# Attention output turned by DMA in bf16 and normalised one unit at a time, with GpSimd's time counted by the program

## The chip, the cores and the metric

The kernel runs on one core of one Trainium2 chip. The metric is the device time of one execution in microseconds (us). The engines that matter are TensorE (PE; its weight loads are PEld), VectorE (DVE), ScalarE (ACT), GpSimd (POOL), and the queue of SyncE (SP), from which every DMA of this kernel is issued.

## The reference

One transformer block without biases, in bf16, for 2048 tokens of width 512: an attention block with 32 heads of 16 columns, then a gated FFN of width 1792. Both start with a layer norm and end with a residual addition.

```python
def _A_ref(x, wqkv, wo):                       # x: (1, 2048, 512), already normalised
    qkv = (x @ wqkv).reshape(B, S, 3, H, Dh).transpose(2, 0, 3, 1, 4)   # H = 32, Dh = 16
    q, k, v = qkv[0], qkv[1], qkv[2]
    scores = jnp.einsum("bhqd,bhkd->bhqk", q, k) * (Dh ** -0.5)
    p = softmax(scores, axis=-1)
    o = jnp.einsum("bhqk,bhkd->bhqd", p, v)
    return o.transpose(0, 2, 1, 3).reshape(B, S, D) @ wo

def _B_ref(x, w_gate, w_up, w_down):           # F = 1792
    return (gelu_tanh(x @ w_gate) * (x @ w_up)) @ w_down

h  = x + _A_ref(layernorm(x), A_wqkv, A_wo)
h2 = h + _B_ref(layernorm(h), B_w_gate, B_w_up, B_w_down)
```

## The kernel before, in words

**Units, groups and ticks.** The queries are cut into 8 groups of 256 tokens (`gi`, 0 to 7; `GL` = 7 is the last), the heads into 8 slots of 4 heads. A unit is one group and one slot; there are 64 (`NU`), in the order of the groups. One Python loop writes the program in ticks. A unit has 16 ticks, so the first 1024 ticks carry the first pass over the scores and the last ones, up to tick 1048, the rest of the second pass, which runs 24 ticks behind (`P2_START`). All engines get fixed lists; waits are semaphores that the planner (`Plan`) puts in.

**First pass.** In each tick TensorE makes two score tiles of 128 queries by 512 keys (L797) and VectorE takes their row maxima in one reduction of 128x1024 elements (L806). GpSimd folds the maxima of a unit: a part after the second and the third quarter of the keys (`negm_part`, emitted in ticks 8 and 12 of the unit), the rest in tick 15 (`negm_pre`, L832 to L840), which leaves the negative maxima as three bf16 rows in `ST`. `negm_post` turns them with a DMA transpose (L846, `STG<-ST`) and, `ADDX` = 4 ticks later, GpSimd adds them to the rows of Q that carry the maximum (L851). Tick 24 of the unit is the first that reads them.

**Second pass.** In each tick TensorE makes two transposed score tiles of 128 keys (L867), and ScalarE evaluates exp into the ring of probability tiles (L896; in the last 24 ticks two tiles at once, L884). `item_pv` (L910) multiplies by V, to which a column of ones is attached, so the sum of the exponentials comes out as 17th row of each head.

**What becomes of a unit's output before.** `item_pv` ends in ticks 8 to 11 of a unit. ScalarE copies its bank to `OA` in fp32. After every second unit `item_ofin` runs: TensorE turns the pair in four fp32 transposes (L936), ScalarE copies the 17 columns of each head to `OAT`, and GpSimd takes the reciprocal of the sums as a power of -1 (L945, `LINV`) and multiplies (L949) into `Otok`. `slot_done` counts the slots; when a group has its eight, `post_onT` turns `Otok` by DMA for the output projection `item_oproj` (L1015); then follow a layer norm from sums (Square on ScalarE, L1029; GpSimd, L1039 to L1053), a DMA transpose (`post_hnT`, L1005) and, three ticks later, the group's FFN is queued: seven pairs of `item_gate` and `item_up` (L1089, 16 matmuls for a pair) and two `item_down` (L1139, 14 matmuls and the residual L1144), one for each 128 tokens.

**The dense stream.** All these items (`Dense`) go through one generator that adds a piece in each tick: items with a due time (`prio`: PV, turning, output projection) first, FFN items in their order. A piece is two to four matmuls' worth; where a tick has less, dummy matmuls (L1299) fill it. A gate or up may start only where an estimate of ScalarE's lag is at most `LAG_START` and where it ends before the next due item. The estimate grows by the cost given to each copy or tangent and falls in each tick:

```python
def act_tick(exps):
    act_lag[0] = max(0.0, act_lag[0] + 0.478 * exps - 1.135)      # exps is 2
```

A copy of a gate or up counts 0.48, a tangent 0.54, a copy of `OA` 0.41, one of `OAT` 0.3. The Gelu of a gate is spread over engines (`gelu_chain`): three GpSimd operations (L1079 to L1081), two ticks later (`TANH_LAG`) a Tanh on ScalarE (L1072), put off tick by tick while the lag is over `LAG_OP`, two more GpSimd operations (L1077, L1078), and the product with the up tile into `GUT` (L1131). There are two sets of buffers, so a gate waits for the product of the gate two before it.

**GpSimd's stream.** `PoolStream` is a list in order; in each tick it may emit as much as a budget of 1.19 allows, and what the program puts on GpSimd directly is taken off (`spend`). Operations over 2.0 (the reciprocal of a pair counts 2.9) are held back in ticks 1 to 3 and 13 to 15 of a unit.

**The end.** From tick 1024 on VectorE is free and takes the copies. The second `item_down` of group 6 is held back until the ticks are over. Then `tail_b` finishes group 7: the last slot's output, output projection and layer norm, with whatever dense work is left as filler (`fill(2)` and `fill(13)`; a piece of `item_down` counts 3, the whole 15), then whatever is still left, and then group 7's seven gate and up pairs with Gelu on ScalarE, and its two down projections.

## Time and profile before

| | before |
|---|---|
| time, median of 3 (lowest, highest) | 1243.8 us (1243.76, 1245.08) |
| the profiled execution's own time | 1243.51 us |
| its span in the profile | 1241.8 us |
| DVE busy | 1188.9 us (96%) |
| ACT busy | 1199.5 us (97%) |
| PE busy | 1137.1 us (92%) |
| POOL busy | 764.4 us (62%) |
| granted clock of TensorE | 1.00 |

The span is what the profiler recorded on the core; 1.7 us of the execution's time lie around it. Busy time counts an instruction from its start to the end of its writes, and the next one of the same engine may begin before that, so ACT and DVE look fuller than their work is: the spacing of equal instructions in a row tells the cost of one.

### The profile page before, as it was taken

What the parts mean: (1) busy time and instruction counts of PE and PEld (TensorE: products, weight loads), DVE (VectorE), ACT (ScalarE), POOL (GpSimd) and SP (SyncE); (2) the same over time, 40 slices, a digit from 0 to 9 for tenths busy, and PEclk for the clock granted to TensorE, in tenths of its full rate; (3) what the DMA queues carried; (4) which work ended last, traced back from release to release, by engine and by line L of the source; (5) the groups of instructions that cost most, each with busy time, mean ns of one, the idle gap of its engine ahead of it and who ended that gap; (6) DMA issues with size and microseconds to landing.
All of it is one profiled execution on the core that took longest, in us unless ns stands there. A gap on an engine that the chain in (4) does not pass through costs nothing.

```text
span 1241.8 us, 31457 instructions
## 1 busy us (share of the span) xinstructions
PE 1137.1 (92%) x12700; PEld 438.6 (35%) x12700; DVE 1188.9 (96%) x1087; ACT 1199.5 (97%) x2444; POOL 764.4 (62%) x1540
## 2 busy tenths in 40 slices
PE   8999888899999999999999998999999999999989
PEld 3333222233333333333333333333333333333335
DVE  8999999999999999999999999999999999999933
ACT  7899999999999999999999999999999999999992
POOL 8557774467746765476645777367654767547760
PEclk9999999999999999999999999999999999999999
DMA  5101004300010000100010000100002000100000
GB/s 151 31 22 28 24 19 125 93 5 4 6 31 12 6 6 6 38 5 6 4 27 18 3 6 6 27 17 6 6 4 36 10 4 6 27 19 3 6 12 18
DMA packets 50800, 27.45 MB, mean 22 GB/s; under 512 B 36064, under 2 KB 49632, under 8 KB 50656
## 3 DMA queue, kind: packets, MB, share of 16 engines
q1 hardware_dynamic: 50656, 25.45, 8.3%
q8 instruction: 101, 1.65, 0.6%
q14 instruction: 43, 0.35, 0.1%
HBM read 11.80 MB, written 2.10 MB: 11 GB/s over the span
## 4 chain that ended last, share of the span: by engine, by line
DVE 60%; ACT 27%; PE 10%; POOL 2%; issue 1%; DMA 1%; POOLq 0%
DVE PM L806 60%; ACT PTM L896 14%; ACT PTG L896 4%; ACT PTE L896 3%; PE pbank L1139 2%; PE pbank L797 1%; PE pbank L867 1%; PE pbank L1089 1%; ACT th_sb L1072 1%; PE pbank L739 1%; ACT g_sb L641 1%; ACT OnT L1029 1%; PE pbank L427 1%; PE pbank L676 1%; DMA STG<-ST 1%
## 5 line engine op out<-in xcount | busy, mean ns | idle before, releaser
L806 DVE TENSOR_REDUCE PM<-pbank 128x2 f32<-128x1024 f32 x1024 | 1162.5, 1213 | 5.9 <-PE pbank L867 3.3
L896 ACT ACTIVATE PTM<-pbank 128x512 bf16<-128x512 f32 x1357 | 721.0, 668 | 4.7
L867 PE MATMUL pbank<-QT,KT 32*128 32x256 bf16 x4096 | 495.2, 273 | 12.2 <-ACT PTM L896 5.1
L797 PE MATMUL pbank<-KT,QT 32*128 32x512 bf16 x2048 | 394.2, 382 | 46.4 <-DVE PM L806 23.8
L1299 PE MATMUL pbank<-ones_bf,ident 128*128 128x512 bf16 x814 | 250.8, 384 | 27.3 <-ACT PTM L896 2.4
L797 PEld LDWEIGHTS pbank<-KT,QT 32*128 32x128 bf16 x2048 | 104.4, 91 | 392.5 <-DVE PM L806 170.3
L896 ACT ACTIVATE PTG<-pbank 128x512 bf16<-128x512 f32 x407 | 221.4, 660 | 0.8
L867 PEld LDWEIGHTS pbank<-QT,KT 32*128 32x128 bf16 x4096 | 163.6, 92 | 66.2 <-ACT PTM L896 34.7
L896 ACT ACTIVATE PTE<-pbank 128x512 bf16<-128x512 f32 x236 | 135.5, 668 | 0.8
L910 PE MATMUL pbank<-PTM,VA 128*17 128x256 bf16 x2776 | 125.7, 274 | 2.8 <-ACT PTM L884 0.9
L832 POOL TENSOR_TENSOR MX<-PM,MX 128x8 f32<-128x8 f32 x64 | 12.9, 202 | 163.6 <-DVE PM L806 163.6
L1299 PEld LDWEIGHTS pbank<-ones_bf,ident 128*128 128x128 bf16 x814 | 49.4, 97 | 132.5 <-ACT PTM L896 82.7
L945 POOL TENSOR_TENSOR LINV<-OAT,negone 128x16 f32<-128x16 f32 (+1 forms) x32 | 92.7, 2896 | 0.0
L910 PEld LDWEIGHTS pbank<-PTM,VA 128*17 128x17 bf16 x2776 | 59.8, 89 | 47.2 <-issue 29.8
L821 POOL TENSOR_TENSOR MX<-PM,MX 128x8 f32<-128x8 f32 x64 | 13.0, 203 | 101.6 <-DVE PM L806 101.5
L1089 PE MATMUL pbank<-hnT_l,wu_sb 128*128 128x256 bf16 x448 | 66.7, 275 | 3.1 <-ACT PTM L896 0.2
L1089 PE MATMUL pbank<-hnT_l,wg_sb 128*128 128x256 bf16 x448 | 66.9, 275 | 2.4
L1078 POOL TENSOR_TENSOR th_sb<-th_sb,g_sb 128x512 f32<-128x512 f32 x49 | 62.2, 1269 | 4.1
L1081 POOL TENSOR_TENSOR th_sb<-th_sb,g_sb 128x512 f32<-128x512 f32 x49 | 62.1, 1268 | 3.1
L1131 POOL TENSOR_TENSOR GUT<-th_sb,u_sb 128x512 bf16<-128x512 f32 x49 | 62.3, 1271 | 2.0
L1079 POOL TENSOR_TENSOR th_sb<-g_sb 128x512 f32<-128x512 f32 x49 | 51.0, 1041 | 19.2 <-ACT g_sb L641 19.2
L1139 PE MATMUL pbank<-wd_sb,GUT 128*128 128x512 bf16 x224 | 60.2, 382 | 0.6 <-ACT PTM L896 0.2
(154 smaller groups left out, 1100.0 us busy)
## 6 DMA issues: line engine op xcount, KB each, us to landing
QKS<-QKS SPq DMA_DIRECT2D x27, 112.0 KB, 2.2
x_sb<-in_A_x_dram SPq DMA_DIRECT2D x4, 512.0 KB, 5.7
xres<-in_A_x_dram SPq DMA_DIRECT2D x16, 128.0 KB, 2.2
out_dram<-out_sb SPq DMA_DIRECT2D x16, 128.0 KB, 1.9
wg_sb<-in_B_w_gate_dram SPq DMA_DIRECT2D x4, 448.0 KB, 5.2
wu_sb<-in_B_w_up_dram SPq DMA_DIRECT2D x4, 448.0 KB, 6.1
wd_sb<-in_B_w_down_dram SPq DMA_DIRECT2D x3, 512.0 KB, 5.5
STG<-ST SPq DMA_TRANSPOSE x64, 2.3
```

Source lines behind the costliest of these rows:

```text
L797: P.op("pe", lambda e, g=g, b=b: e.matmul(pbank[:, b, :], QT[32 * g:32 * g + 32, c, slot, 128 * qt:128 * qt + 128], KT[32 * g:32 * g + 32, ...
L806: P.op("dve", lambda e: e.tensor_reduce(out=PM[:, par, qt, kc, g:g + 2], in_=pbank[:, b:b + 2, :], axis=AX.X, op=ALU.max), reads=[("pb", b ...
L867: P.op("pe", lambda e, kt=kt, i=i: e.matmul(pbank[:, b, 256 * i:256 * i + 256], KT[32 * g:32 * g + 32, slot, 128 * kt:128 * kt + 128], QT[ ...
L896: P.op("act", lambda e, b=b, pi=pi: e.activation(out=PTt(pi), in_=pbank[:, b, :], func=ACT.Exp), reads=[("pb", b)], writes=[("PT", pi)], e ...
L910: P.op("pe", lambda e, g=g, kt=kt, pi=pi, i=i: e.matmul(pbank[32 * g:32 * g + 17, b, 0:256], VA[:, kt, 4 * slot + g, :], PTt(pi)[:, 256 * ...
L945: P.op("pool", lambda e: e.tensor_tensor(out=li, in0=oat4[:, :, :, 16], in1=negone[:, 0:8 * ns].rearrange("p (q h) -> p q h", q=2), op=ALU ...
L1078: o(1.27, lambda e: e.tensor_tensor(out=ts_, in0=ts_, in1=gs, op=ALU.mult), [("th", par), ("g", par)])], then=done)
L1081: o(1.27, lambda e: e.tensor_tensor(out=ts_, in0=ts_, in1=gs, op=ALU.mult), [("th", par), ("g", par)])], then=lambda: defer(TANH_LAG, lamb ...
L1089: P.op("pe", lambda e, dc=dc, fc=fc, i=i: e.matmul(pbank[:, b, 256 * i:256 * i + 256], w[:, dc, 128 * fc:128 * fc + 128], hT[:, dc, :], st ...
L1131: P.op("pool", lambda e: e.tensor_tensor(out=o_ap, in0=shp(ts_), in1=shp(us), op=ALU.mult), reads=[("th", par), ("u", par)], writes=o_keys ...
L1139: P.op("pe", lambda e: e.matmul(pbank[:, b, :], GUT[:, fc, 128 * k:128 * k + 128], wd_sb[:, fc, :], start=first, stop=last), reads=[("GUT" ...
L1299: P.op("pe", lambda e: e.matmul(pbank[:, b, :], ident[:], ones_bf[:, 0:512], start=True, stop=True), reads=["ident", "ones_bf"], writes=[( ...
```

## The change

The output of each unit goes another way from PSUM to `Otok`. ScalarE copies it to `OB` in bf16; `o_turn` turns it with a DMA transpose (`OBT<-OB`, on SP's queue); five ticks later `o_norm` puts the reciprocal and the multiplication of this one unit on GpSimd's stream. `item_ofin` with its TensorE transposes and the copy to `OAT` is left for one unit only, the last but one. The very last unit is normalised in `tail_norm` as before.

GpSimd's stream has a second count, `t`, of when GpSimd will have done what was given to it (`charge`, with durations in `TOOK` and a tick of 1.135 us). A reciprocal is emitted in tick 0 of a unit, right behind the rows of the maxima, whatever the budget, and held back in ticks 1 to 3 and 12 to 15. The rows of the maxima are now emitted at the head of tick 16 rather than at the end of tick 15 (`unit_end`), with `ADDX` = 3, so that the addition to Q stays in the same tick; the parts move from ticks 8 and 12 to 9 and 13. A tangent is put off until GpSimd's count says that its input will be ready (`poly_end`, `POLY`), and while a gate or up is being made its copy counts as lag already (`LAG_TH`). `LAG_START` goes from 0.4 to 0.3. `post_onT` and `post_hnT` are issued in ticks 5 to 14 of a unit only (`clear`).

```diff
-ADDX = 4
+ADDX = 3
...
-LAG_START = 0.4
+LAG_START = 0.3
...
+POLY = 1.3
+TICK = 1.135
+TOOK = {1.04: 1.13, 0.62: 0.7, 1.27: 1.26, 1.45: 1.67, 0.31: 0.4}
+LAG_TH = 0.2
...
+            def charge(self, took, ready=0.0):
+                self.t = max(self.t, TICK * dense.now, ready) + took
+                return self.t
             def run(self, flush=False):
-                while self.q and (flush or self.budget >= min(self.q[0][0], 1.0)):
-                    if not flush and self.q[0][0] > 2.0 and dense.now % 16 in (1, 2, 3, 13, 14, 15):
+                while self.q and (flush or self.budget >= min(self.q[0][0], 1.0) or (self.q[0][1].__name__ == 'inv' and dense.now % 16 == 0)):
+                    if not flush and self.q[0][1].__name__ == 'inv' and dense.now % 16 in (1, 2, 3, 12, 13, 14, 15):
                         break
                     cost, fn, then = self.q.pop(0)
                     self.budget -= cost
+                    self.charge(TOOK.get(cost, cost))
...
-            defer(ADDX, add)
+            defer(ADDX + (ui == NU - 1), add)
...
-            evac_act(OA[:, par, 256 * col:256 * col + 256], pbank[:, b, 0:256], [("pb", b)], [("OA", par, col)], cost=0.41)
             if gi == GL and slot >= NSLOT - 2:
+                evac_act(OA[:, par, 256 * col:256 * col + 256], pbank[:, b, 0:256], [("pb", b)], [("OA", par, col)], cost=0.27)
                 if col == 0:
-                    dense.add(item_ofin, gi, (slot,), front=True, est=3, not_before=dense.now + 3)
-            elif col == 1:
-                dense.add(item_ofin, gi, (slot - 1, slot), front=True, est=3, not_before=dense.now + 3)
+                    dense.add(item_ofin, gi, front=True, est=3, not_before=dense.now + 3)
+            else:
+                evac_act(OB[:, ui % 2, :], pbank[:, b, 0:256], [("pb", b)], [("OB", ui % 2)], cost=0.27, then=lambda: o_turn(ui))
...
+        def o_turn(ui):
+            gi, slot = units[ui]
+            par = ui % 2
...
+            P.dma("sp", lambda e: e.dma_start_transpose(out=OBT[:, par, :, :], in_=OB[:, par, :]), ("obT", par), reads=[("OB", par)], writes=[("OBT", par)])
+            o4 = OBT[:, par].rearrange("p q (g i) -> p q g i", i=32)
+            defer(5, lambda: o_norm(gi, slot, par, o4, ("OBT", par), ob_busy))
+
+        def o_norm(gi, slot, par, o4, key, busy):
...
+            def inv():
+                P.op("pool", lambda e: e.tensor_tensor(out=li, in0=o4[:, :, :, 16], in1=negone[:, 0:8].rearrange("p (q h) -> p q h", q=2), op=ALU.pow),
+                     reads=[key, "negone"], writes=[("LINV", par)])
+            o_ap = Otok[:, :, 64 * slot:64 * slot + 64].rearrange("p q (h i) -> p q h i", i=16)
+            def mul():
+                P.op("pool", lambda e: e.tensor_tensor(out=o_ap, in0=o4[:, :, :, 0:16], in1=li.unsqueeze(3).broadcast_to([128, 2, 4, 16]), op=ALU.mult),
+                     reads=[key, ("LINV", par)], writes=[("Otok", slot)])
...
+            pool.add([(1.45, inv), (0.31, mul)], then=over)
...
+        def clear(fn):
+            if not force[0] and not 5 <= dense.now % 16 <= 14:
+                defer(1, lambda: clear(fn))
+            else:
+                fn()
...
-                    defer(5 + k, lambda k=k: post_onT(gi, k))
+                    defer(5 + k, lambda k=k: clear(lambda: post_onT(gi, k)))
...
-                defer(1, lambda: pool.add(ln2_from_sums(gi, k, t), then=lambda: defer(2, lambda: post_hnT(gi, k))))
+                defer(1, lambda: pool.add(ln2_from_sums(gi, k, t), then=lambda: defer(2, lambda: clear(lambda: post_hnT(gi, k)))))
...
             def later(n):
-                if not force[0] and act_lag[0] > LAG_OP + 0.1 * n:
+                if not force[0] and (act_lag[0] + (0.48 if dense.gen is not None and dense.cur in (item_gate, item_up) else 0) > LAG_TH + 0.1 * n or poly_end[par] > TICK * dense.now + POLY):
                     defer(1, lambda: later(n + 1))
                     return
...
+            def poly_done():
+                poly_end[par] = pool.t
+                defer(TANH_LAG, lambda: later(0))
...
+        def unit_end(ui):
+            pool.spend(1.8)
+            st_end[0] = pool.charge(2.0, TICK * (16 * ui + 15) + 2.35)
+            negm_pre(ui)
+            negm_post(ui)
...
+            if tick and tick % 16 == 0 and p1_ok:
+                unit_end(tick // 16 - 1)
...
-                if tick % 16 in (8, 12):
+                if tick % 16 in (9, 13):
                     pool.spend(0.7)
-                    negm_part(tick // 16, 1 if tick % 16 == 8 else 2)
-                if tick % 16 == 15:
-                    pool.spend(1.8)
-                    negm_pre(tick // 16)
-                    negm_post(tick // 16)
+                    pool.charge(0.9 if tick % 16 == 9 else 1.2, TICK * tick + 1.3)
+                    negm_part(tick // 16, 1 if tick % 16 == 9 else 2)
+                if tick == 16 * NU - 1:
+                    unit_end(tick // 16)
```

More of the change, by code (lines that the diff above doesn't have):

```diff
@@ new lines, in o_norm, with over @@
+        def o_norm(gi, slot, par, o4, key, busy):
+            assert gi < 1 or otok_consumed.get(gi - 1), "dense stream too far behind (Otok reuse)"
+            li = LINV[:, par, 0:8].rearrange("p (q h) -> p q h", q=2)
+            def inv():
[5 more added lines that the diff above has]
+                     reads=[key, ("LINV", par)], writes=[("Otok", slot)])
+            def over():
+                busy[par] = False
+                slot_done(gi, (slot,))
+            pool.add([(1.45, inv), (0.31, mul)], then=over)
@@ L956, in item_ofin @@
+        def item_ofin(b, gi):
+            slot = NSLOT - 2
+            for q in range(2):
+                P.op("pe", lambda e, q=q: e.transpose(out=pbank[:, b, 128 * q:128 * q + 128], in_=OA[:, 1, 128 * q:128 * q + 128], identity=ident32[:]),
+                     reads=[("OA", 1, 0), "ident32"], writes=[("pb", b)], sig=(q == 1))
             v17 = lambda ap: ap.rearrange("p (qh i) -> p qh i", i=32)[:, :, 0:17]
-            evac_act(OAT[:, par, 0:136 * ns].rearrange("p (qh i) -> p qh i", i=17), v17(pbank[:, b, 0:256 * ns]), [("pb", b)], [("OAT", par)], then=norm, cost=0.3)
@@ L958, in item_ofin @@
-            return 1
+            evac_act(OAT[:].rearrange("p (qh i) -> p qh i", i=17), v17(pbank[:, b, 0:256]), [("pb", b)], ["OAT"],
+                     then=lambda: o_norm(gi, slot, 1, OAT[:].rearrange("p (q h i) -> p q h i", q=2, i=17), "OAT", {}), cost=0.3)
+            return 1
+            yield
+        def clear(fn):
[3 more added lines that the diff above has]
+                fn()
         out_n = [0]
```

41 lines of the change are left out of this document (14 added, 27 removed).

## The prediction

> **What bounds the kernel now.** I read the page first, then VectorE's timeline, then the last 60 us engine by engine and along the chain of waits.
>
> ```profile
> span 1241.8 us, 31457 instructions
> L806 DVE TENSOR_REDUCE PM<-pbank 128x2 f32<-128x1024 f32 x1024 | 1162.5, 1213 | 5.9 <-PE pbank L867 3.3
> L832 POOL TENSOR_TENSOR MX<-PM,MX 128x8 f32<-128x8 f32 x64 | 12.9, 202 | 163.6 <-DVE PM L806 163.6
> ```
>
> The row maxima alone fill 1162.5 of 1241.8 us, and in all of the first pass VectorE stood idle ahead of them for 5.9 us. So nothing in the change can shorten the 1024 ticks by more than that, however much it takes off ScalarE, TensorE or GpSimd. VectorE's timeline shows where the idle time lies (in brackets: idle before, and who ended it):
>
> ```profile
> 33.38 336.52 DVE L806 TENSOR_REDUCE PM<-pbank 128x2 f32<-128x1024 f32 x296 [0.75 <-PE pbank L797]
> ...
> 1099.52 5.75 DVE L806 TENSOR_REDUCE PM<-pbank 128x2 f32<-128x1024 f32 x5 [0.29 <-PE pbank L867]
> 1105.45 80.53 DVE L806 TENSOR_REDUCE PM<-pbank 128x2 f32<-128x1024 f32 x71 [0.17 <-PE pbank L867]
> ```
>
> 0.75 us of it lies ahead of 33.38, before the first second-pass tile, so 5.1 us at most can be had. Later gaps are of 0.17 and 0.29 us. A tick is 80.53/71 = 1.13 us, and the last reduction ends at 1105.45 + 80.53 = 1185.98. What follows, 56 us up to the span's end, has no VectorE bound, and is where the time must come from. ScalarE there, then GpSimd:
>
> ```profile
> 1195.33 0.64 ACT L1072 ACTIVATE th_sb<-th_sb 128x512 f32<-128x512 f32 x1
> 1195.86 1.94 ACT L884 ACTIVATE PTM<-pbank 128x1024 bf16<-128x1024 f32 x2
> 1198.38 0.63 ACT L1072 ACTIVATE th_sb<-th_sb 128x512 f32<-128x512 f32 x1 [0.58 <-POOL th_sb L1081]
> ```
>
> ```profile
> 1187.97 2.93 POOL L945 TENSOR_TENSOR LINV<-OAT,negone 128x16 f32<-128x16 f32 x1
> ...
> 1191.56 0.67 POOL L851 TENSOR_TENSOR QT<-QT,STG 128x256 bf16<-128x256 bf16 x1
> ...
> 1197.08 1.27 POOL L1081 TENSOR_TENSOR th_sb<-th_sb,g_sb 128x512 f32<-128x512 f32 x1
> ...
> 1200.25 0.62 POOL L1077 TENSOR_SCALAR th_sb<-th_sb 128x512 f32<-128x512 f32 x1
> 1200.95 1.27 POOL L1078 TENSOR_TENSOR th_sb<-th_sb,g_sb 128x512 f32<-128x512 f32 x1
> ...
> 1203.40 1.65 POOL L945 TENSOR_TENSOR LINV<-OAT,negone 128x8 f32<-128x8 f32 x1
> 1205.13 0.40 POOL L949 TENSOR_TENSOR Otok<-OAT,LINV 128x128 bf16<-128x128 f32 x1
> 1205.49 1.27 POOL L1131 TENSOR_TENSOR GUT<-th_sb,u_sb 128x512 bf16<-128x512 f32 x1
> ```
>
> ScalarE is the bound from 1186 to 1210 (the last exponentials end, in the chain below, at 1206.45 + 3.67 = 1210.12): double exponentials back to back, with two tangents of group 6 between them, and it stood before the second for 0.58 us because GpSimd's third Gelu operation ended only at 1198.35. Before that GpSimd had spent 2.93 us on a pair's reciprocal. Then the chain of waits:
>
> ```profile
> 1206.45 3.67 ACT PTM L884 x4
> ...
> 1213.81 2.37 PE pbank L1139 x11
> ...
> 1217.05 0.45 PE pbank L1224 x8
> 1217.49 0.43 PE pbank L1144 x2
> 1217.93 2.37 PE pbank L1139 x11
> 1220.52 5.24 PE pbank L1089 x48
> ```
>
> ```profile
> 1217.31 0.62 DVE L1232 COPY hnT_l<-pbank 128x512 bf16<-128x512 bf16 x2 [0.34 <-PE pbank L1224]
> ```
>
> This is the costliest thing to see. Both down projections of group 6 (L1139) are still there in the tail. The first (3 + 11 matmuls, and 3 of the second) fills TensorE's time during the last layer norm, which is useful. The other 11 and the residual stand between the last normalised transposes (1217.05) and the first gate of group 7 at 1220.52, although VectorE has delivered that gate's operand at 1217.31 + 0.62 = 1217.93. These 2.59 us are in nobody's shadow.
>
> **The change part by part.** The pace of group 6's FFN, from the rows of single lines in the window 1060 to 1215 us, and one more of VectorE's timeline:
>
> ```profile
> L641 ACT ACTIVATE g_sb<-pbank x6: 603/642/754, 1113.9 to 1185.3; 128x512 f32<-128x512 f32 x6
> L641 ACT ACTIVATE out_sb<-pbank x2: 604/621/638, 1079.2 to 1099.3; 128x512 bf16<-128x512 f32 x2
> L1029 ACT ACTIVATE OnT<-xres x2: 631/684/738, 1096.8 to 1102.6; 128x512 bf16<-128x512 bf16 x2
> L1005 SPq DMA_TRANSPOSE hnT_l<-OnT x2: 1193/1194/1196, 1101.7 to 1107.1; - x2
> ...
> 1188.98 0.69 DVE L630 COPY g_sb<-pbank 128x512 f32<-128x512 f32 x1 [0.84 <-PE pbank L1089]
> ```
>
> *Pace.* Six intervals of gates from 1113.9 to 1188.98 are 12.5 us each, 11.0 ticks. The program's own account explains it: a tick gives back 1.135 - 2 x 0.478 = 0.179, a unit 2.86; outputs take 0.41 and half of 0.3 of it; a gate and up pair takes 2 x 0.48 + 0.54 = 1.50. So (2.86 - 0.56)/1.50 = 1.53 pairs fit a unit, one in 10.4 ticks, and 95% of that is reached. After, outputs take 0.27 only: 1.73 pairs, one in 9.3 ticks, 9.8 at 95%. `LAG_START` 0.3 and the 0.48 counted ahead of tangents cost part of it. Walking the new rules by hand from the first gate to the seventh, I come to 63 ticks (10.5 each) against 66.
>
> *Start.* The copy of group 5's second down (1099.3) lies between the two Squares (1096.8, 1102.6) and by the lag rule holds the second back 0.48/0.179, about 3 ticks. With FFNs ending earlier and four turning items less in a group, both downs fit ahead of the output projection, so the FFN starts 3 to 4 ticks earlier. Together the last gate of group 6 comes 7 ticks, 8 us, earlier: at about 1181 instead of 1188.98.
>
> *End of group 6's Gelu.* Its last polynomial operation then follows the last maxima, which end at 1188.0 (where the reciprocal started in before): 1188.0 + 1.27 = 1189.3. Tangent to about 1190.6; GpSimd meanwhile does reciprocal, multiplication and addition, 1.65 + 0.40 + 0.67, to 1192.0; then 0.62 + 1.27 + 1.27 to 1195.2. In the program the first down can start at tick 1038, between due items; the 24 last ticks took 1185.98 to 1210.1, 1.0 us each, so this is near 1200, and it needs five ticks and must be in before the last PV at tick 1045. The products are ready 5 us before. Then `fill(2)` and `fill(13)`, together 15, hold exactly the second down (five pieces of 3), and nothing is left over: 2.59 us go, less the start of the first gate behind 1217.93, for which I leave 0.1. **-2.5 us.** What is late next is VectorE's copy of the transposes.
>
> *Tangents.* One tangent instead of two among the last exponentials, and its input is 1 us early: its spacing, 1195.86 - 1195.33 = 0.53, and the wait of 0.58. **-1.1 us.**
>
> *ScalarE, TensorE in the first pass.*
>
> ```profile
> L641 ACT ACTIVATE OAT<-pbank 128x272 f32<-128x272 f32 x31 | 13.1, 422 | 0.0
> L936 PE MATMUL pbank<-ident,OA 128*128 128x128 f32 x126 | 27.6, 301 | 0.0
> ```
>
> 30 copies to `OAT` go, 30 x 0.42 = 13 us of ScalarE, and 124 transposes, 27 us of TensorE, where dummies take their room. VectorE covers both: 0. The copy to `OB` has the shape of that to `OA`; I count it the same. Of the 5.1 us of gaps, the 0.29 and 0.17 pair stands where output projections and Squares of a group end meet (1099.5 lies between the Squares), and this meeting stays. Isolated ones of 0.17 may go with fewer copies: **-0.5 us**, with 5.1 gained as one end; new gaps are a rival.
>
> *GpSimd.* 62 single reciprocals instead of 31 pairs: 62 x (1.65 + 0.40) = 127 us, against 31 x (2.93 + 0.62, reading the multiplication of a pair as an L1077) = 110. 17 us more on an engine that waits 163.6 us for the maxima's last part alone: 0. The multiplication and reciprocal now stand between the maxima's rows and the addition to Q; the 2.93 did so in before. Moving the rows' emission by a tick costs nothing for the same 163.6: they wait for VectorE anyway. If that cover went, L851 would be late for second-pass tiles five ticks on.
>
> *SP.*
>
> ```profile
> STG<-ST SPq DMA_TRANSPOSE x64, 2.3
> ```
>
> 62 DMA transposes of the size of `STG` are added on SP's queue. Each waits there for ScalarE's copy in ticks 8 to 11; behind it are queued the group's transposes, weight pieces, and `STG` in tick 16, at least five ticks later. It lands in about 2.3 us; the reciprocal comes five to seven ticks, 5.7 us at least, after it. 0. If the copy were late, `STG` and with it Q would be.
>
> The Trainium skill, page "VectorE: DVE Perf Modes", section "Rules for kernel authors", says to turn 128x128 on TensorE where PSUM will do as destination, and by DMA otherwise; its table beside gives 390 ns against 1309 ns. By that rule this turning is a step back of an estimated 0.9 us a block. The trace agrees in the order (301 ns against 2.3 us), but here the later landing is hidden by 5.7 us.
>
> *`clear`.* `post_hnT` falls, by my walk, on ticks 6 and 8 of its unit, `post_onT` on 6 and 7, inside the window: 0.
>
> Sum: -2.5 - 1.1 - 0.5 = -4.1 on the profiled execution's 1243.5, which is 1.7 over its span: 1239.4. The median of the runs, 1243.8, is 0.3 above it: **1239.7 us**.
>
> **The rivals.**
> *The down stays (same).* If GpSimd's count or `LAG_START` slow the gates so that the last product comes after tick 1039, both downs remain. For: the margin is some 5 ticks out of 89, and I walked a schedule by hand. Against: pace and start both gain. Then at most 1.1 + 0.5 is left: 1242.2.
> *`clear` catches the transposes (slower).* Place: the second `post_hnT` of group 6. From tick 15 of its unit it waits to tick 5 of the next, then for the PV there, so 10 to 13 ticks go. It decides from a slip of 7 ticks. With later slips on top, more than 15 ticks in all, a gate and up pair falls behind the exponentials: 48 gate and up matmuls take 5.24 us, so 1.7 for a pair at least, and up to 6.7 if its Gelu (1.04 to 1.27 an operation) is waited for. +4 in the middle: 1247.8. Against: by my walk both lie six ticks and more ahead of the window's end, and in before they were only 5.4 us apart.
> *Gaps (slower).* Denser gates and tangents crowd ScalarE and open new gaps of 0.17 to 0.29 us in the maxima. It decides from (2.5 + 1.1)/0.17, some 21 gaps; if each of the 49 pairs opened one it is 49 x 0.17 = 8.3 more: 1248.5. Against: tangents are put off more readily than before.
> *The DMA turn is late (slower).* Landing over 5.7 us instead of 2.3 would stop GpSimd in front of L851. Against: the queue is nearly empty then. +1 to +5: 1247.
>
> **How the numbers follow.** Forecast 0.64, own range 1237.5 to 1241.2; the down stays 0.17; `clear` 0.08; gaps 0.08; the turn 0.03. A difference of 0.2%, 2.5 us, is about what a measurement of this kernel can tell. Faster by more: the forecast and a little of the second, 0.66. Same: most of the second and the mild ends of the slower ones, 0.19. Slower: 0.15. Range 1236.5 (more of the 5.1 gone) to 1245.0; it leaves out the slower cases and no more than 0.05 below.
>
> **What would show it.** Right: L1139 x14 with its residual between exponentials before 1206; only one group of L1139 behind 1210; the first L1089 x48 some 0.1 us behind VectorE's L1232; one tangent after the last reduction, no idle before it; gaps ahead of L806 still 4 to 6 us. Wrong: two down projections after the last exponential, reductions ending past 1187, or L851 waiting long for `STG`.

## The result and the profile after

| | before | after |
|---|---|---|
| time, median (lowest, highest; 20 runs each) | 1243.72 us (1242.84, 1245.16) | 1241.25 us (1240.03, 1242.41) |
| the profiled execution's own time | 1243.51 us | 1240.54 us |
| its span | 1241.8 us | 1238.8 us |

The change makes the kernel faster by 2.5 us: the ratio is 0.998, with a 95% interval of 0.9973 to 0.9986. The forecast was 1239.7 us, with 1237.5 to 1241.2 as its own range: the time lies 1.6 us above the one and just above the other. Rows of the page of the kernel after (line numbers from here on are those of the kernel after; L806 has become L818, L867 L880, L1072 L1098, L1089 L1118, L1139 L1170, L851 L864, L945 L957):

```profile
span 1238.8 us, 31200 instructions
PE 1083.9 (87%) x12422; PEld 420.9 (34%) x12620; DVE 1188.7 (96%) x1085; ACT 1195.0 (96%) x2415; POOL 776.8 (63%) x1602
L818 DVE TENSOR_REDUCE PM<-pbank 128x2 f32<-128x1024 f32 x1024 | 1163.8, 1213 | 5.3 <-PE pbank L880 2.4
L957 POOL TENSOR_TENSOR LINV<-OBT,negone 128x8 f32<-128x8 bf16 x62 | 103.3, 1666 | 0.0
L1118 PE MATMUL pbank<-hnT_l,wg_sb 128*128 128x256 bf16 x448 | 67.0, 275 | 6.0 <-DMA hnT_l<-OnT 4.5
L864 POOL TENSOR_TENSOR QT<-QT,STG 128x256 bf16<-128x256 bf16 x64 | 42.7, 668 | 40.1 <-DMA STG<-ST 40.1
```

TensorE's busy time fell by 53 us and ScalarE's by 4.5, GpSimd's rose by 12, and nearly none of it reached the time, because VectorE's maxima still fill the span. One row is new: TensorE now stands 4.5 us ahead of gates until a DMA has brought `hnT_l`. VectorE's timeline of the kernel after tells where the time went (in brackets: idle before, and who ended it):

```profile
33.10 637.70 DVE L818 TENSOR_REDUCE PM<-pbank 128x2 f32<-128x1024 f32 x561 [0.75 <-PE pbank L809]
672.25 11.40 DVE L818 TENSOR_REDUCE PM<-pbank 128x2 f32<-128x1024 f32 x10 [1.45 <-PE pbank L880]
684.06 425.40 DVE L818 TENSOR_REDUCE PM<-pbank 128x2 f32<-128x1024 f32 x374 [0.40 <-PE pbank L880]
1109.64 11.40 DVE L818 TENSOR_REDUCE PM<-pbank 128x2 f32<-128x1024 f32 x10 [0.19 <-PE pbank L880]
1121.45 65.14 DVE L818 TENSOR_REDUCE PM<-pbank 128x2 f32<-128x1024 f32 x57 [0.40 <-PE pbank L880]
...
1204.41 0.69 DVE L642 CAST out_sb<-pbank 128x512 bf16<-128x512 f32 x1 [5.71 <-PE pbank L1175]
...
1216.61 0.62 DVE L1263 COPY hnT_l<-pbank 128x512 bf16<-128x512 bf16 x2 [0.17 <-PE pbank L1255]
```

These rows cut the span into three parts that every kernel of this study shares. The first is what lies ahead of the reduction at 33.10, the thirteenth, behind which the gaps end that all kernels have at the beginning. The second is the 1012 reductions from there (561 + 10 + 374 + 10 + 57) to the last one's end, 1121.45 + 65.14 = 1186.59: 1153.49 us. The third is the rest of the span, 52.21 us. The kernel before has 33.38, 1152.60 and 55.82. So the tail gave 3.61 us, the 1012 reductions took 0.89 back, and the beginning gave 0.28 (it is 32.8 to 34.0 us in the 14 kernels, so this is no more than their spread). The same parts for all kernels:

| kernel | 1012 reductions | rest after them | median | ratio to before (95%) |
|---|---|---|---|---|
| before | 1152.60 | 55.82 | 1243.72 | 1 |
| after | 1153.49 | 52.21 | 1241.25 | 0.998 (0.9973, 0.9986) |
| e1_ffn_6 | 1148.32 | 52.64 | 1235.75 | 0.9942 (0.9928, 0.9955) |
| e2_ffn_2 | 1160.45 | 52.14 | 1247.17 | 1.0029 (1.0019, 1.0039) |
| e3_hold_down | 1153.10 | 54.68 | 1243.14 | 0.9998 (0.9989, 1.0007) |
| e4_old_tangent | 1153.74 | 52.10 | 1241.65 | 0.9984 (0.9975, 0.9992) |
| e5_old_rows | 1150.41 | 52.16 | 1238.03 | 0.9946 (0.9934, 0.9959) |
| e6_turn_only | 1157.90 | 51.65 | 1245.20 | 1.0008 (0.9999, 1.0017) |
| e7_turn_only_6 | 1158.63 | 52.02 | 1246.18 | 1.0013 (1.0005, 1.0022) |
| e8_turn_only_6_lag3 | 1176.10 | 52.72 | 1263.89 | 1.0157 (1.0143, 1.0171) |
| e9_all_6_lag4 | 1154.08 | 52.49 | 1241.85 | 0.9983 (0.9975, 0.9992) |
| e10_6_lag25 | 1149.78 | 52.62 | 1237.70 | 0.9951 (0.9939, 0.9964) |
| e11_ffn_4 | 1151.40 | 52.22 | 1238.11 | 0.9955 (0.9943, 0.9968) |
| e12_ffn_5 | 1149.23 | 52.69 | 1236.81 | 0.9945 (0.9932, 0.9959) |

The first two columns are worked out in this way from VectorE's timeline of one profiled execution; each ratio is against the kernel before on the same chip (its medians there: 1243.3 to 1244.3).

**The tail.** ScalarE, GpSimd and TensorE at the end of the kernel after:

```profile
1190.45 0.68 ACT L1098 ACTIVATE th_sb<-th_sb 128x512 f32<-128x512 f32 x1
1190.97 9.33 ACT L897 ACTIVATE PTM<-pbank 128x1024 bf16<-128x1024 f32 x10
```

```profile
1188.58 1.26 POOL L1110 TENSOR_TENSOR th_sb<-th_sb,g_sb 128x512 f32<-128x512 f32 x1
1189.80 1.67 POOL L957 TENSOR_TENSOR LINV<-OBT,negone 128x8 f32<-128x8 bf16 x1
...
1192.87 0.67 POOL L864 TENSOR_TENSOR QT<-QT,STG 128x256 bf16<-128x256 bf16 x1 [0.93 <-DMA STG<-ST]
...
1195.56 1.27 POOL L1162 TENSOR_TENSOR GUT<-th_sb,u_sb 128x512 bf16<-128x512 f32 x1
```

```profile
1203.99 0.38 PE L1175 MATMUL pbank<-xres,ident 128*128 128x512 bf16 x1
...
1213.12 2.54 PE L1170 MATMUL pbank<-wd_sb,GUT 128*128 128x512 bf16 x11
1215.49 0.38 PE L1175 MATMUL pbank<-xres,ident 128*128 128x512 bf16 x1
...
1216.94 0.38 PE L1175 MATMUL pbank<-xres,ident 128*128 128x512 bf16 x1
1217.35 1.03 PE L1118 MATMUL pbank<-hnT_l,wg_sb 128*128 128x256 bf16 x8
```

One tangent is left behind the last reduction, and no idle time stands before it. The first down of group 6 is done among the exponentials (its residual at 1203.99, its copy at 1204.41), the second is TensorE's filler behind them, and the first gate starts at 1217.35, 0.12 us behind VectorE's copy (1216.61 + 0.62 = 1217.23).

**The new wait.** The waits of the kernel after that name `hnT_l`'s DMA (us in total, times, longest):

```profile
PEld pbank L1118 <- DMA hnT_l<-OnT: 6.2, 6, 2.5
PE pbank L1118 <- DMA hnT_l<-OnT: 4.5, 6, 2.2
```

The kernel before has no such wait. Six is the number of groups whose FFN follows its transposes at once (all of the first pass but group 0). For group 3, the chain of waits and TensorE's timeline of the kernel after:

```profile
656.11 0.21 POOL MX L844
...
658.09 1.60 POOL LINV L957
...
666.15 0.77 POOL OnT L1078
...
666.94 4.29 DMA hnT_l<-OnT
671.23 0.05 issue
671.28 0.61 PE pbank L1118 x4
```

```profile
671.28 0.61 PE L1118 MATMUL pbank<-hnT_l,wg_sb 128*128 128x256 bf16 x4 [2.21 <-DMA hnT_l<-OnT]
```

TensorE came to the gate 2.21 us before its operand landed, at 671.28 - 2.21 = 669.07, 2.1 us after the DMA's issue at 666.94. The score tiles queued behind the gate waited with it, and VectorE stood 1.45 us at 672.25 and 0.40 us ten ticks on. The same part of the kernel before, by line 1005 in the window 655 to 680 us, and by TensorE's timeline:

```profile
L1005 SPq DMA_TRANSPOSE hnT_l<-OnT x2: 1190/1193/1196, 663.9 to 669.2; - x2
...
DMA to landing us min/median/max: 2.4/2.4/2.4
```

```profile
673.83 0.61 PE L1089 MATMUL pbank<-hnT_l,wg_sb 128*128 128x256 bf16 x4
```

There the second transpose was issued at 669.2 and landed at 671.6; the gate at 673.83 stood 2.2 us behind it and cost nothing. The change brought the transpose forward by 2.3 us, and TensorE's turn to take the gate by 4.8.

### The profile page after: what moved, and what is told of

It reads as the page before. It is cut to its first block, busy times and chain, and to the rows that moved or that the text cites. A ratio compares the mean times of both kernels' runs of the same rounds, so it can differ in the third digit from the quotient of the medians.

```text
span 1238.8 us, 31200 instructions
## 1 busy us (share of the span) xinstructions
PE 1083.9 (87%) x12422; PEld 420.9 (34%) x12620; DVE 1188.7 (96%) x1085; ACT 1195.0 (96%) x2415; POOL 776.8 (63%) x1602
## 3 DMA queue, kind: packets, MB, share of 16 engines
q8 instruction: 101, 1.65, 0.6%
## 4 chain that ended last, share of the span: by engine, by line
DVE 55%; ACT 25%; POOL 9%; PE 6%; issue 3%; DMA 2%; POOLq 0%; DVEq 0%
DVE PM L818 54%; ACT PTM L909 14%; ACT PTG L909 4%; POOL LINV L957 3%; ACT PTE L909 3%; DMA hnT_l<-OnT 1%; PE pbank L1118 1%; ACT th_sb L1098 1%; ACT u_sb L653 1%; ACT g_sb L653 1%; PE pbank L880 1%; PE pbank L923 1%; PE pbank L809 1%; POOL OnT L1078 1%; POOL rstd L1075 1%
## 5 line engine op out<-in xcount | busy, mean ns | idle before, releaser
L818 DVE TENSOR_REDUCE PM<-pbank 128x2 f32<-128x1024 f32 x1024 | 1163.8, 1213 | 5.3 <-PE pbank L880 2.4
L909 ACT ACTIVATE PTM<-pbank 128x512 bf16<-128x512 f32 x1357 | 731.2, 703 | 8.5 <-PE pbank L880 1.9
L880 PE MATMUL pbank<-QT,KT 32*128 32x256 bf16 x4096 | 499.5, 273 | 11.9 <-ACT PTM L909 3.2
L1330 PE MATMUL pbank<-ones_bf,ident 128*128 128x512 bf16 x696 | 222.1, 383 | 75.1 <-ACT PTM L909 41.8
L809 PEld LDWEIGHTS pbank<-KT,QT 32*128 32x128 bf16 x2048 | 99.5, 91 | 384.6 <-DVE PM L818 162.1
L909 ACT ACTIVATE PTG<-pbank 128x512 bf16<-128x512 f32 x407 | 225.9, 690 | 2.0 <-PE pbank L880 0.6
L880 PEld LDWEIGHTS pbank<-QT,KT 32*128 32x128 bf16 x4096 | 163.5, 92 | 70.6 <-ACT PTM L909 39.7
L909 ACT ACTIVATE PTE<-pbank 128x512 bf16<-128x512 f32 x236 | 138.6, 706 | 1.1
L957 POOL TENSOR_TENSOR LINV<-OBT,negone 128x8 f32<-128x8 bf16 x62 | 103.3, 1666 | 0.0
L1118 PE MATMUL pbank<-hnT_l,wg_sb 128*128 128x256 bf16 x448 | 67.0, 275 | 6.0 <-DMA hnT_l<-OnT 4.5
L844 POOL TENSOR_TENSOR MX<-PM,MX 128x8 f32<-128x8 f32 x64 | 12.8, 200 | 93.0 <-DVE PM L818 92.7
L1118 PE MATMUL pbank<-hnT_l,wu_sb 128*128 128x256 bf16 x448 | 67.1, 275 | 2.2
L864 POOL TENSOR_TENSOR QT<-QT,STG 128x256 bf16<-128x256 bf16 x64 | 42.7, 668 | 40.1 <-DMA STG<-ST 40.1
```

Of the source, the lines that this page charges most:

```text
L809: P.op("pe", lambda e, g=g, b=b: e.matmul(pbank[:, b, :], QT[32 * g:32 * g + 32, c, slot, 128 * qt:128 * qt + 128], KT[32 * g:32 * g + 32, ...
L818: P.op("dve", lambda e: e.tensor_reduce(out=PM[:, par, qt, kc, g:g + 2], in_=pbank[:, b:b + 2, :], axis=AX.X, op=ALU.max), reads=[("pb", b ...
L880: P.op("pe", lambda e, kt=kt, i=i: e.matmul(pbank[:, b, 256 * i:256 * i + 256], KT[32 * g:32 * g + 32, slot, 128 * kt:128 * kt + 128], QT[ ...
L909: P.op("act", lambda e, b=b, pi=pi: e.activation(out=PTt(pi), in_=pbank[:, b, :], func=ACT.Exp), reads=[("pb", b)], writes=[("PT", pi)], e ...
L957: P.op("pool", lambda e: e.tensor_tensor(out=li, in0=o4[:, :, :, 16], in1=negone[:, 0:8].rearrange("p (q h) -> p q h", q=2), op=ALU.pow), ...
L1118: P.op("pe", lambda e, dc=dc, fc=fc, i=i: e.matmul(pbank[:, b, 256 * i:256 * i + 256], w[:, dc, 128 * fc:128 * fc + 128], hT[:, dc, :], st ...
```

## The experiments

After this comparison there were three theories for the 1.4 us that lie between the forecast's part in the first pass (-0.5) and the measured one (+0.89). *Landing*: the FFN of a group is queued so early that the first gate waits for the transpose, and the first pass would be shorter than before without that. *Clock*: the granted clock, 0.997 to 1.0 in the runs of the kernel after, costs the time by itself. *Pattern*: denser gates and tangents crowd ScalarE, as the prediction's third rival had it. Where the expectations name theories by letters, A is the landing, B the clock and C the pattern.

**Queue the FFN later, and earlier.** In the kernel after, one number:

```diff
-                defer(3, lambda: add_ffn_when(gi))
+                defer(6, lambda: add_ffn_when(gi))      # e2: 2, e11: 4, e12: 5
```

> The changed kernel, but a group's FFN is queued 6 ticks after its second hnT transpose is issued, not 3. Theory A (landing): in the changed kernel the first gate of each group waits on TensorE for that transpose to land, and where it lands late (4.3 us in group 3 of the profiled execution) VectorE runs dry for 1 to 2 us. Then the waits at the first gates go (10.7 us of idle TensorE weight loads behind the DMA in the changed kernel, under 1 here), the gap of 1.45 us and its like in the maxima go, the last gate of group 6 still leaves the first down ahead of the last PV, and the time is 1238.7 to 1239.7, a ratio to before of about 0.9964. Theory B (clock): what is missing comes from a TensorE clock granted at 0.997 to 0.999 in most executions, because TensorE has less to do: then the clock stays there and the time stays near 1241.2. Theory C (ScalarE crowded by denser gates and tangents): the gaps move but their sum stays, 1241 to 1242.

> The other way: the FFN is queued 2 ticks after the second hnT transpose is issued, one tick earlier than in the changed kernel; gate 6 and the downs of group 6 stay in the ticks that they have. Theory A: each group's first gate stands a tick (1.13 us) longer for the landing, beyond what VectorE's two tiles in hand cover: 0.5 to 1.1 us in each of six or seven groups, 1244 to 1249. Theories B and C: no change beyond 0.5 us, 1241.2.

Six ticks: 1235.75 us, ratio 0.9942; two ticks: 1247.17, 1.0029. Three ticks of delay, at first sight a loss for an FFN that has to be done in time, gain 0.38% by the two ratios, 4.7 us (5.5 by the medians). That is the way that the landing theory said, and some 3 us more than it had priced. VectorE's timeline of e1 has one row for all 1012 reductions, and TensorE's has the gate of group 3 with no wait before it, at nearly the same time as in the kernel after:

```profile
32.84 1148.32 DVE L818 TENSOR_REDUCE PM<-pbank 128x2 f32<-128x1024 f32 x1012 [0.75 <-PE pbank L809]
```

```profile
671.32 0.61 PE L1118 MATMUL pbank<-hnT_l,wg_sb 128*128 128x256 bf16 x4
```

Against after's 671.28 the gate started no later, only nothing stood still for it. The tail is about as after's (52.64), so the end of group 6's FFN can bear the delay. With two ticks the waits grow, and each group opens a gap in the maxima; the waits of e2:

```profile
PE pbank L1118 <- DMA hnT_l<-OnT: 8.8, 6, 2.1
```

The clock does not part after from e1: the profiled executions of before, after, e1 and e5 all show 1.000, and after's three runs at 1.0 took 1240.03 to 1240.54 us against 1235.39 to 1236.39 in e1's four. The granted clock was 0.994 to 0.999 in e2's runs and 0.999 to 1.0 in e1's, but also 0.996 to 1.0 in before's and 0.996 to 0.999 in e7's, and these two have no wait for `hnT_l`. So the dips do not go with these waits alone; what sets them is open, and so is how much of the long times of e2, e7 and e8 is theirs.

> The changed kernel with the FFN queued 4 ticks after the second hnT transpose is issued. In the changed kernel (3 ticks) every first gate started within 0.1 us of the landing; one tick, 1.13 us, more should take away the wait in groups whose transpose lands in the usual 2.4 us and leave a rest where it takes 4.3: most of the 3 us that the wait costs in the first pass, so 1238 to 1239.5 if the gates' pattern behind is as in the changed kernel, less if that improves too.

> The same with 5 ticks. From the second gate on, its program is that of the run with 6 ticks (1235.75 us); only the first gate of each group is one tick earlier, which leaves it some 2 us behind an ordinary landing. If the landing alone sets what the first gate costs: 1235.5 to 1236.5, no waits of first gates but for late landings. If the first gate's distance to the units' rows or copies matters beside the landing: 1237 or more.

Four ticks give 1238.11 and five 1236.81. The series 2, 3, 4, 5, 6 is 1247.2, 1241.3, 1238.1, 1236.8, 1235.8 us: 5.9, 3.1, 1.3 and 1.1 for each tick (the kernel before took 1243.3 to 1243.7 beside them). Four ticks came as expected; with five, the time lies between the two that were expected (at most 1236.5, or 1237 and more). At four ticks two waits for the DMA are left, 2.0 us on the weight loads (`PEld`) in all; at five and six, none. So the step from 5 to 6, if there is one (the intervals of the two ratios overlap), is not the landing.

**Take the wait away and leave the schedule.** To part landing from pattern, e5 keeps after's program, but gates and ups of groups 1 to 6 read the buffer of the group before, which has long landed (so the FFN of these groups is computed from other rows, and the output is not the block's):

```diff
-            hT = hnT_l[gi % 2]
-            hr = [("hnT", gi % 2, k) for k in range(2)] if gi != GL else [("hnT", gi % 2, 0), ("hnTx", 0), ("hnTx", 2)]
+            sg = (gi - 1 if 0 < gi < GL else gi) % 2
+            hT = hnT_l[sg]
+            hr = [("hnT", sg, k) for k in range(2)] if gi != GL else [("hnT", gi % 2, 0), ("hnTx", 0), ("hnTx", 2)]
```

> The changed kernel, FFN queued after 3 ticks as in it, but the gates and ups of groups 1 to 6 read the normalised rows of the group before (the other hnT buffer, landed long ago), so that no first gate waits for a landing; the instructions, their order and ticks are the same, and the output is that of other rows. The run with 6 ticks was 5.5 us faster than the changed kernel, twice what the gaps at the landings in the profiled execution add up to (2.5 us). If all of it is the wait for the landing (on TensorE, and what it sets back on ScalarE behind it): 1235.5 to 1236.5, and the small periodic gaps in the maxima go with it. If half is the pattern of the first gates (gates at offsets 956 and 962, tangents and copies close together on ScalarE): 1238 to 1239, and the gaps of about 0.1 to 0.2 us at ticks 71, 102 and 103 of each 128 stay.

It took 1238.03 us, ratio 0.9946. VectorE's timeline of e5:

```profile
33.73 1150.41 DVE L818 TENSOR_REDUCE PM<-pbank 128x2 f32<-128x1024 f32 x1012 [0.75 <-PE pbank L809]
```

The wait alone is worth 1153.49 - 1150.41 = 3.08 us of the profiled execution (by the two ratios 0.34%, 4.2 us, each known to about 0.1%). That shows the wait for the landing as the cause of the loss. The other 1150.41 - 1148.32 = 2.09 us between e5 and e1 lie in no gap long enough for a row: the reductions follow each other in 1.1368 us here (1150.41/1012) and in 1.1347 in e1.

The start of each reduction in the three traces tells where both shares lie. The median spacing is 1.131 us in all. Counted from 0 in each group of 128, reductions 61 and 71 come later than that by 3.36 us in all in after, by 0.25 in e5 and by nothing in e1: this is the landing. Reductions 91, 102, 103 and 123 come later by 2.72 us in after, 2.74 in e5 and 0.27 in e1, with the same 0.17 us at 103 in each of the last six groups of after and of e5. These small gaps stay when the wait is taken away and go with the later FFN, much as the expectation's second case had it; they are the pattern's share. The size of it stands on two profiles; the ratios, 0.9946 and 0.9942, do not part e5 from e1.

**Put the first down back.** To weigh the tail's largest term, e3 holds both downs of group 6 back until the ticks are over:

```diff
-            if it[0] is item_down and it[1] == (GL - 1, 1) and not force[0]:
+            if it[0] is item_down and it[1][0] == GL - 1 and not force[0]:
```

> The changed kernel with both downs of group 6 held back until the ticks are over, as only the second is now; nothing else differs. The prediction's largest term says that the first down, pulled in among the last exponentials, is worth 2.5 us, because filler then takes up exactly the second: so 2.5 us slower than the changed kernel, 1243.7, and 11 L1170 matmuls and the residual once more between VectorE's copy of the transposes and group 7's first gate. Rival: the gate of group 7 was late for another reason; then under 1 us.

It took 1243.14 us (ratio 0.9998 against after's 0.998), with a rest of 54.68 us against 52.21. The chain of waits of e3:

```profile
1216.44 0.38 PE pbank L1175
1216.82 2.37 PE pbank L1170 x11
1219.19 0.22 PE pbank L1175
1219.41 5.24 PE pbank L1118 x48
```

The eleven matmuls stand again between the transposes and the first gate: 2.47 us, where the prediction had 2.5. The tail's other 54.68 - 55.82 = -1.14 is what the prediction gave to the tangent; no run takes that alone. By the medians' ratios the first down is worth 0.18%, 2.2 us.

**The old rule for tangents.**

```diff
-                if not force[0] and (act_lag[0] + (0.48 if ... else 0) > LAG_TH + 0.1 * n or poly_end[par] > TICK * dense.now + POLY):
+                if not force[0] and act_lag[0] > LAG_OP + 0.1 * n:
```

> The changed kernel with the old rule for when a tangent is emitted (lag over 0.2 + 0.1 n only: no count of GpSimd's time, no copy counted ahead). Only one tangent is left behind the last reduction in both, one tick earlier here. If the gain at the end came from the earlier FFN and not from the rule, the end is the same within 0.6 us. In the first pass tangents come up to 2 ticks earlier: if ScalarE then waits for GpSimd, idle time ahead of L1098 goes up from nearly nothing by 1 to 5 us and a part of it shows as gaps in the maxima, +0.5 to +2 us; if the rule does nothing, 1241.2.

1241.65 us, ratio 0.9984 against 0.998: no difference that can be measured, and the tail is the same (52.10). So it isn't the tangents' own rule that took the second tangent out of the tail. What remains is the earlier FFN, and that it is this was not tried alone. Tangents wait for GpSimd's polynomial for 1.0 us here, the low end of what was expected.

**The turn without the counting.** e6 has the DMA turn and the normalisation of one unit alone; `ADDX`, `LAG_START` (0.4), the places of the maxima's parts and rows, the order on GpSimd and the rule for tangents are those of before, without `clear`. One rule of before has no effect there: a single reciprocal counts 1.45, so the hold of operations over 2.0, which caught the reciprocal of a pair, never holds it. e7 is e6 with the FFN after 6 ticks.

> The DMA turn and the normalisation of single units alone: ADDX 4, LAG_START 0.4, parts of the maxima in ticks 8 and 12, their rows at the end of tick 15, no reciprocal ahead of its budget, the old tangent rule, no holding of transposes. By the program, gate 6 of group 6 then falls on tick 1009 and the first down on 1038, so the end should keep its 3.6 us and win another 0.5 for the second tangent. The first gates follow the transposes as in the changed kernel and wait for the landing too. If the rest of the change is worth nothing: 1240.5 to 1241.5. If the rest (rows and reciprocals placed by GpSimd's time, tangents when ready) is what keeps ScalarE and the additions to Q in time: 1243 or more.

> The same, the turn alone, with the FFN queued after 6 ticks. Against the changed kernel with 6 ticks (1235.75) it shows what the other parts bring where the landing is out of the way: 1235 to 1236.5 if nothing, 1237 to 1240 if they keep gaps away. Waits of first gates for the landing should be near 0 as there.

They took 1245.20 and 1246.18 us: e6 in its second case, e7 6 us above both of its cases. Both have the short tail (51.65 and 52.02), so the tail's gain belongs to the turn. But their 1012 reductions take 5.3 and 6.0 us longer than before's. The page of e6:

```profile
L818 DVE TENSOR_REDUCE PM<-pbank 128x2 f32<-128x1024 f32 x1024 | 1164.3, 1214 | 9.3 <-PE pbank L880 7.0
```

One thing was expected of e6 that did not come: its first gates do not wait for the landing, though its FFN too is queued after three ticks. Its GpSimd and TensorE in group 3:

```profile
655.36 1.67 POOL L957 TENSOR_TENSOR LINV<-OBT,negone 128x8 f32<-128x8 bf16 x1
658.79 0.20 POOL L844 TENSOR_TENSOR MX<-PM,MX 128x8 f32<-128x8 f32 x1 [1.76 <-DVE PM L818]
...
667.13 0.77 POOL L1078 TENSOR_SCALAR OnT<-xres,rstd,nmr 128x512 bf16<-128x512 bf16 x1
```

```profile
671.78 0.60 PE L1118 MATMUL pbank<-hnT_l,wg_sb 128*128 128x256 bf16 x4
```

The second transpose is issued at 667.93 and the gate stands 3.85 us behind it (3.84 to 3.85 in groups 1 to 6); in after TensorE comes to it after 2.1. In e6 the reciprocal is done ahead of the last part of the maxima (L844), while GpSimd would wait for VectorE. From there to the end of the second layer norm it is 667.90 - 658.79 = 9.1 us. In after the reciprocal stands behind the rows of the maxima, and the same stretch is 666.92 - 656.11 = 10.8 us. The 1.7 us between the two are the reciprocal's 1.67, and the 1.7 us that the gate lost on the transpose. So by these rows the wait for the landing came with the new place of the reciprocal; that place was not tried alone.

The other half of the change, which alters the order of work and holds reciprocals back again, is worth 1157.90 - 1153.49 = 4.4 us with 3 ticks, its own wait for the landing taken off, and 1158.63 - 1148.32 = 10.3 with 6. Which of its rules does it was tried for one of them, the tangents' (e4), and `LAG_START`:

```diff
-LAG_START = 0.4
+LAG_START = 0.3       # e8: in e7;  e9: 0.4 in e1;  e10: 0.25 in e1
```

> The turn alone with the FFN queued after 6 ticks, as in the run that took 1246.2 us, and with LAG_START 0.3 instead of 0.4: gates and ups start at a lower lag of ScalarE. If the gaps that the turn alone opens in the maxima (its chain of waits runs through ScalarE: copies of gates and ups with a tangent right behind) come from ScalarE being given too much at once, this one number takes most of them away: 1237 to 1240. If they come from GpSimd's order (maxima and reciprocals), the rest of the change is needed and this stays at 1244 to 1246.

> The whole change with the FFN queued after 6 ticks (1235.75 us) and LAG_START back at 0.4. The other side of the same question: if ScalarE's crowding at the gates is what matters, 3 to 8 us slower, 1239 to 1244; if the counted tangents and GpSimd's order already keep it in time, within 1 us of 1235.75.

> The whole change with the FFN after 6 ticks and LAG_START 0.25, to see whether there is more to be had in the same direction: the first pass has about 1.5 us of gaps behind tick 40 left in the run with 0.3. Gate 6 of group 6 falls one tick later, the first down stays at tick 1038. 1235 to 1236.5.

This was the surprise of the study. With the other half of the change, 0.3 in place of 0.4 gains 1241.85 - 1235.75 = 6.1 us (5.1 by the ratios); without it, the same number costs 1263.89 - 1246.18 = 17.7 (17.9), where one case had expected a gain and the other nothing. And 0.25 took 1237.70 us, where 1235 to 1236.5 were expected: no gain over 0.3, and 1 to 2 us of loss if any. The waits of e8 and two stretches of its GpSimd timeline:

```profile
ACT th_sb L1098 <- POOL th_sb L1110: 13.7, 16, 1.6
```

```profile
997.38 1.04 POOL L1108 TENSOR_TENSOR th_sb<-g_sb 128x512 f32<-128x512 f32 x1 [2.79 <-ACT g_sb L653]
...
1001.52 1.67 POOL L957 TENSOR_TENSOR LINV<-OBT,negone 128x8 f32<-128x8 bf16 x1
1003.16 0.20 POOL L844 TENSOR_TENSOR MX<-PM,MX 128x8 f32<-128x8 f32 x1
...
1008.45 0.67 POOL L864 TENSOR_TENSOR QT<-QT,STG 128x256 bf16<-128x256 bf16 x1 [1.96 <-DMA STG<-ST]
...
1009.90 1.26 POOL L1110 TENSOR_TENSOR th_sb<-th_sb,g_sb 128x512 f32<-128x512 f32 x1
```

ScalarE stood 13.7 us before tangents (3.0 in e7, so this is 10.7 of the 17.7), since GpSimd still had the polynomial to do: at 1001.52 a reciprocal goes ahead of the maxima's rows, these end late, the addition to Q waits for their DMA, and the polynomial, behind it in the list, ends only at 1011.16. The kernel after has no wait of a tangent for the polynomial at all in its waits. A likely reason, not shown: gates that start only where ScalarE's lag is small leave it so small that a tangent is never put off by lag; then only the count of GpSimd's time and the order of its list keep the tangent from being issued too early. e4, which has 0.3 and the order but not the count, waits only 1.0 us, so it points to the order; with six ticks the two were not tried apart.

The best kernel of the study is e1: the whole change with the FFN after six ticks, 1235.75 us, ratio 0.9942, 7.6 us faster than before on the same chip. Whether the counting and the six ticks bring as much with the turn left on TensorE was not tried.

## Why the prediction was right, and where not

**Bound.** Right. VectorE's maxima remained the bound, and the tail and the gaps moved the time, though TensorE was busy for 53 us less.

**The tail, -2.5 and -1.1.** Right: 3.61 measured, 2.47 and 1.14 by e3. That it agrees to 0.1 us is partly luck, since the tails of the kernels that have the short one spread from 51.65 to 52.72. The steps: the polynomial's end at 1189.84 (forecast 1189.3), the products at 1195.56 + 1.27 = 1196.83 (1195.2; the addition to Q waited 0.93 us for `STG`, which I had not counted), the first down before 1204.4 (before 1206), the filler of 15 used up by the second down, the gate 0.12 us behind the copy (0.1). The tangent's new rule has no part in it, as e4 showed; pace and start, by which it was worked out, are these:

**Pace and start.** One row for each end of the kernel after's gate copies of group 6, from ScalarE's timeline:

```profile
1110.66 0.61 ACT L653 ACTIVATE g_sb<-pbank 128x512 f32<-128x512 f32 x1
...
1182.81 0.71 ACT L653 ACTIVATE g_sb<-pbank 128x512 f32<-128x512 f32 x1
```

The first is 3.2 us earlier than in before (forecast 3 to 4 ticks, 3.4 to 4.5 us), the last 63.5 ticks of 1.136 us later (forecast 63), at 1182.81 (about 1181). The start holds the wait for the landing in group 6, about 1 us.

**GpSimd, 0.** Right in amount: 62 reciprocals at 1.67 us, forecast 1.65; 12 us more busy, forecast 17. Wrong in place: the prediction weighed the reciprocal behind the rows of the maxima only against the addition to Q. The layer norms stand behind it too, and so does the transpose that the first gate waits for (e6 above). L851's successor L864 waits for `STG` twice as long as before, 40.1 us against 20.1, at most 2.6 at a time; this was named as a sign of being wrong, but no row shows a delay from it other than those 0.93 us.

**SP and the turn.** Right that it is hidden: `OBT` lands in 2.3 us in the median and 4.2 at most, and no reciprocal waits for it (idle 0.0 in the row of L957). By the rule of the Trainium skill (page "VectorE: DVE Perf Modes", section "Rules for kernel authors") and the table of that page, the turn is a step back of an estimated 0.9 us a block, 56 us for 62 blocks if each stood in the path. e6, which has the turn and the normalisation of single units without the other rules, is within 0.2% of before.

**The first pass, -0.5: wrong.** It was +0.89, and this is the 1.4 us that the forecast is off by in the profiled execution (the beginning's -0.28 apart). The step that failed is what was made of "so the FFN starts 3 to 4 ticks earlier". The FFN did (the first gate of group 3 starts when 571 reductions are over in e5 and in e6, 574 in before), and I booked it as a gain for the tail. I took the transposes only as to whether `clear` or SP's queue would hold them, and did not set the new place of the first gate against the landing of its own operand, which has no term in the sum. The rows for it were there: issue at 669.2, 2.4 us to land, gate at 673.83, so 2.2 us of slack in before, less than the 3 to 4 ticks that I took off. What this leaves out is that the transpose comes earlier too. In e6 the two moved so that 3.85 us are left between issue and gate, which is enough; in after 2.1 are left, since GpSimd does the reciprocal and both layer norms (658.09 to 666.92) ahead of the transpose, as one list in order. The price of the wait was 3.08 us (e5); without it the first pass would have been 2.2 us shorter than before's, more than the 0.5 forecast. So two things that the forecast had not priced, 1.7 us of gain and 3.1 of loss, stand against each other in its 1.4, and it is luck that it is off by no more. The prediction's third rival, gaps, came about in a small measure, but mostly by a mechanism that it didn't name.

**The other rivals.** The down didn't stay, `clear` caught no transpose of group 6 (its last gate would have been ten ticks late), and the turn was not late.

## What to carry to other kernels

When a change starts a consumer earlier, set its new place against the landing of every one of its operands, DMA ones first, and not only against the engine that it frees: the slack in the profile of before is the most that can be taken off for nothing. Look as well at what the same change puts ahead of the engine that makes the operand. In a stream of fixed lists a wait of one early item is paid by all that is queued behind it, so putting an item later can make the whole faster, and a sweep of the one delay (here 2 to 6 ticks, 11 us from end to end) is the cheapest test for it. A threshold that was tuned with other rules has to be tried again with the new ones: the same step from 0.4 to 0.3 took off some 5 to 6 us with one order of the other engines' work and added 18 with another.

## What the runs showed of the hardware

The two DMA transposes of one operand, equal in size and from the same queue, did not take the same time: 2.4 us from issue to landing in before's group 3, and 4.29 us for the second in after's (the longest in before is 4.4). Line 1030 of the kernel after in the window 655 to 680 us (shortest, median and longest in ns on the queue):

```profile
L1030 SPq DMA_TRANSPOSE hnT_l<-OnT x2: 1195/1820/2444, 663.8 to 666.9; - x2
```

The longer one was 2444 ns on the queue in place of 1195, with no other DMA of SP's queue shown in that time (the next one, `OBT`'s, follows at 669.43). But transfers of two other queues, which the view calls `instruction`, ran in it; the DMA view of after from 666.94 to 669.38 us:

```profile
q8 instruction: 1, 0.02, 3.7%
q14 instruction: 1, 0.01, 2.1%
```

The same view of before's transpose, 669.22 to 670.41, has none. Over the traces of all 14 kernels, 1673 DMA transposes had no transfer of an `instruction` queue beside them, and none of these took more than 1.29 us on the queue; 421 had one for some of their time, and 141 of these took more than 1.5 us. So every long one met such a transfer. That the transfer is the cause is not shown, and why 280 others met one and stayed short is open. A transpose whose reader is placed by its median landing can thus be 1.9 us late.
